# Ten unread products on TensorE between the opening's spectrum and the first steps back

## The chip, the cores and the metric

The kernel runs on one core of a Trainium2 chip. The time is that of one execution on the device, in microseconds (us). Before the change five runs gave a median of 1884.59 us (1883.99 to 1885.54). A profile is one further execution with the hardware profiler on; its own time is given beside it.

## The reference

A spectral filter over a sequence, followed by a feed-forward block with a softmax-like gate:

```python
# x (8, 3136, 256), filt_r and filt_i (1569, 256)
X = np.fft.rfft(x, axis=1)
Y = X * (filt_r + 1j * filt_i)[None, :, :]
x = np.fft.irfft(Y, n=3136, axis=1).reshape(25088, 256)

h = x @ w_in                                    # (25088, 1024)
sm = exp(h - max(h)) / (sum(exp(h - max(h))) + 1e-9)
solu = h * sm
ln = (solu - mean(solu)) / sqrt(var(solu) + 1e-6) * g_ln
out = ln @ w_out                                # (25088, 256)
```

All of it is done in 32-bit floats.

## The kernel before, in words

The transform of length 3136 is split as 49 x 64, and each part is done as matrix products with constant tables. For each of the 8 sequences ("entries") there are four steps:

- **first** (L171, product L177, tile `pa`): a table `wf_t` times rows of `x`. ACT copies the result from PSUM to `t` (L180), and DMAs store it to a DRAM scratch `d1`.
- **forward** (L199, product L203, `pb`): rows fetched back from `d1` are multiplied with the table `de`. DVE and ACT then multiply with the filter in `multiply` (L207), which leaves the product tile `p` in `prods`.
- **inverse** (L227, product L233, `pc`): `de` again, times `p`. ACT copies the result to `g` (L236), and `store` (L238) sends it by a DMA of the POOL queue to a second DRAM scratch `d2`.
- **back** (L253, product L258, `py`): `fetch_back` (L245) brings a chunk of `d2` into a tile `t` by two DMAs of the SP queue (L145, L146: 96 rows and 4 rows). A group of four products of 100 rows and 98 columns with the table `wi_t` fills one PSUM tile, which ACT copies into `y` (L261). A chunk gives two groups, one for each half of the 256 channels.

Then the feed-forward block works on blocks of 128 tokens: `h` (L415) from `y` and `w_in_sb`, maximum, exponential and gate on DVE and ACT, a transposition by DVE and DMA, and `po` (L475) with `w_out_sb`.

The program has two stages. The **opening** (L267 to L369) handles entries 0 and 1 alone: all of their first steps, then a loop over 25 units of the spectrum (L354), in which unit i + 1 is started before unit i is inverted, then the back steps of entry 0 in 8 chunks, 16 groups (L362). On DVE it also converts the weights from 64-bit words (L280). The **main stage** (L549 on) runs over 196 token blocks in an order written out by hand, with the transforms of the other entries spread between the blocks; it keeps TensorE full nearly all of its length. Its first rows of `x`, `x_1` and `x_2` among them, are asked for on the SP queue behind the last chunk of the opening's back steps.

PSUM is divided into pools by tag. `h` (two slots of two banks) holds `pa` and `pb` of the opening and `h` of the main stage. `t` (two slots of one bank) holds `pc`, `py` and the main stage's `pa`. So a `py` group needs one of two slots, and gets it when ACT has copied the group before last. In the opening the framework derives the waits from the tiles; instructions of one engine run in the order in which they are queued there. The SP queue, too, is in order: chunks 0 to 5 of the back steps have buffers at once, chunks 6 and 7 wait until chunks 0 and 1 have been used by `py`, and the main stage's rows are queued behind them.

The last store of `d2` in the opening must land before the first chunk can be read back, since every chunk takes rows from all 25 units.

Of the kernel before, what the change touches and what calls it, by code (L numbers as in the profile page):

```python
# [9 lines left out]
FP32 = mybir.dt.float32  # L10
# [7 lines left out]
P = 128  # L18
# [62 lines left out]
def kernel(  # L81
# [10 lines left out]
    nc = tc.nc  # L92
# [5 lines left out]
    def pool(name, bufs, space=None, stack=ctx):  # L98
        kw = {} if space is None else {"space": space}
        return stack.enter_context(tc.tile_pool(name=name, bufs=bufs, **kw))  # L100
# [3 lines left out]
    ps_h = pool("ps_h", 2, PSUM)  # L104
# [19 lines left out]
    de = consts.tile([P, NS, 2, P], FP32, name="de")  # L124
# [142 lines left out]
    with ExitStack() as st:  # L267
# [61 lines left out]
        sp = Spectrum(0, pools, resident)  # L329
        raws = {}  # L330

        def begin(j):
            raws[j] = load_words(weights[j][1], j)
# [13 lines left out]
        def start(i):  # L347
            sp.fetch(i)
            sp.fetch_filter(i)
            sp.forward(i, ps_h.tile([P, 2, 512], FP32, name=f"pb_0_{i}", tag="h").rearrange(  # L350
                "p a (b c) -> p (a b) c", c=C)[:, 0:2, :])

        start(0)
        for i in range(NS):  # L354
            sp.multiply(i)
            if i + 1 < NS:
                start(i + 1)
            sp.inverse(i, nc.scalar.copy)
            sp.store(i, nc.gpsimd.dma_start)
        for j in (4, 5):  # L360
            begin(j)
        for ch in range(NH // NCH):  # L362
# [140 lines left out]
    for g in range(NS // NG):  # L503
        for k, filt in enumerate((filt_r, filt_i)):
            for half in range(2):
                loads[g].append(lambda filt=filt, half=half, k=k, g=g: nc.gpsimd.dma_start(
                    out=f_dram[NG * g:NG * g + NG, 32 * half:32 * half + 32, k, :].rearrange(
                        "s p c -> p s c"),
# [4 lines left out]
    for n in range(1, len(GROUPS)):  # L513
        entries, first_at, spectrum_at = GROUPS[n]
        sp = Spectrum(n, pools, load_filter)
# [15 lines left out]
    for e in range(1, B):  # L531

        start, end = -(-S * (e - 1) // P) + (3 if e == 3 else 1), S * e // P - 1
# [67 lines left out]
```

## Time and profile before

| | |
|---|---|
| median of 5 runs | 1884.59 us (1883.99 to 1885.54) |
| the profiled execution | 1884.83 us |
| its span, first to last instruction | 1882.9 us |
| mean granted clock of TensorE | 0.974 |
| PE busy | 1806.0 us, 96% of the span |
| DVE, ACT, POOL busy | 1112.0, 817.2, 456.5 us |
| DMA | 300.77 MB, 160 GB/s in the mean |
| all `py` products (L258) | 147.8 us |
| all `pa` products (L177) | 144.5 us |

PE is TensorE's row of products, PEld its row of weight loads, which lies beside the products. A 32-bit product appears as two instructions, so a count of x8 on PE is four products of the program. The page cuts the span into 40 slices and gives a digit for each: for an engine the tenths of the slice in which it was busy, for PEclk the clock that TensorE was granted, in tenths of full speed. At half clock every product takes twice as long, and PE counts as busy all that time: a full PE row doesn't say that PE runs at its best, the clock row must be read with it. The ends of products are modelled, and two that follow each other overlap by some 0.2 us; so the pace is read from start to start.

The waits name, for an engine and a line, what ended its idle time. The chain of waits goes back from the last instruction to whatever released each step. A question for stretches of time gives each engine's busy time between two moments, with the granted clock and the share of time in which the 16 DMA engines were busy.

### The profile page before, as it was taken

How to read it: one execution, taken by the hardware profiler on the slowest of the kernel's cores; microseconds unless marked ns; L12 is line 12 of the kernel's file. 1: busy time of each engine (PE TensorE's matmuls, PEld its weight loads, DVE VectorE, ACT ScalarE, POOL GpSimd, SP SyncE). 2: the span in 40 equal slices, each digit the busy share in tenths (PEclk: the TensorE clock that was granted, in tenths of full speed). 3: DMA queues.
4: the chain of work that ended last, by engine and by line, in shares of the span. 5: the costliest groups of instructions: out<-in, count | busy, mean ns of one | idle time of the engine just before them, and what ended most of it. 6: DMA issues, size and time to landing. Idle time of an engine off the chain costs nothing.

```text
span 1882.9 us, 21235 instructions
## 1 busy us (share of the span) xinstructions
PE 1806.0 (96%) x6500; PEld 1167.5 (62%) x6500; DVE 1112.0 (59%) x1778; ACT 817.2 (43%) x1329; POOL 456.5 (24%) x1306
## 2 busy tenths in 40 slices
PE   6678799999999999999999999999999999999997
PEld 1126456666666666666666666666767666666665
DVE  0792455566665655566676655566665655666663
ACT  2373345545545534354545444444444343333331
POOL 3241243332333221132232121213222011110110
PEclk9795899999999999999999999999999999999999
DMA  9875489877787765666657656466675534434434
GB/s 284 255 232 153 142 225 251 233 195 173 185 210 192 200 151 140 144 149 164 169 148 175 157 121 158 103 158 166 155 179 114 116 89 114 112 83 103 101 90 101
DMA packets 314575, 300.77 MB, mean 160 GB/s; under 512 B 27601, under 2 KB 278994, under 8 KB 314464
## 3 DMA queue, kind: packets, MB, share of 16 engines
q1 hardware_dynamic: 283904, 206.69, 47.2%
q0 software_dynamic: 28768, 86.45, 15.3%
q10 hardware_dynamic: 1792, 6.29, 0.9%
q8 instruction: 53, 0.87, 0.2%
q14 instruction: 58, 0.48, 0.1%
HBM read 118.44 MB, written 81.40 MB: 106 GB/s over the span
## 4 chain that ended last, share of the span: by engine, by line
PE 90%; DMA 3%; issue 2%; POOL 1%; DVE 1%; ACT 1%; SPq 0%; POOLq 0%; DVEq 0%; ACTq 0%
PE po L475 36%; PE h L415 35%; PE py L258 7%; PE pa L177 5%; PE pb L203 4%; PE pc L233 3%; DMA x<-in_x_dram 1%; POOL d L241 1%; DMA d<-t 1%; DMA t<-d 1%; DVE nmax L420 0%; ACT e L423 0%; DVE solu L438 0%; ACT t L180 0%; POOL f L310 0%
## 5 line engine op out<-in xcount | busy, mean ns | idle before, releaser
L475 PE MATMUL po<-w_out_sb,solu_t 128*128 128x256 f32 x3136 | 711.8, 380 | 4.5 <-DVE ot L483 4.5
L415 PE MATMUL h<-w_in_sb,y 128*128 128x512 f32 x1568 | 710.1, 596 | 0.0
L475 PEld LDWEIGHTS po<-w_out_sb,solu_t 128*128 128x128 f32 x3136 | 591.7, 190 | 137.9 <-issue 57.0
L420 DVE TENSOR_REDUCE nmax<-h 128x1 f32<-128x1024 f32 x196 | 239.8, 1223 | 455.2 <-PE h L415 455.2
L415 PEld LDWEIGHTS h<-w_in_sb,y 128*128 128x128 f32 x1568 | 295.1, 191 | 317.0 <-issue 306.4
L423 ACT ACTIVATE e<-h,nmax 128x1024 f32<-128x1024 f32 x196 | 218.6, 1115 | 605.8 <-DVE nmax L420 605.8
L440 ACT ACTIVATE e<-solu,nmu 128x1024 f32<-128x1024 f32 x196 | 225.0, 1148 | 293.2 <-DVE solu L438 287.1
L438 DVE SCALAR_TENSOR_TENSOR solu<-e,rsum,h 128x1024 f32<-128x1024 f32 x196 | 251.0, 1280 | 7.1 <-DVE rsum L435 0.3
L448 DVE STREAM_TRANSPOSE turn<-solu 128x1024 f32<-128x1024 f32 x196 | 242.0, 1235 | 0.0
L241 POOL DMA_DIRECT2D d<-g x101 | 76.0, 753 | 565.9 <-ACT g L236 555.5
L258 PEld LDWEIGHTS py<-wi_t,t 100*128 100x128 f32 x1024 | 148.0, 215 | 59.8 <-issue 41.6
L177 PE MATMUL pa<-x,wf_t 98*100 98x512 f32 x256 | 144.5, 675 | 22.9 <-DMA x<-in_x_dram 17.6
L258 PE MATMUL py<-wi_t,t 100*128 100x98 f32 x1024 | 147.8, 297 | 16.6 <-DMA t<-d 9.3
L467 POOL COPY rs_t<-rs 32x1 f32<-32x1 f32 x784 | 141.7, 181 | 35.7
L483 DVE TENSOR_SCALAR ot<-po,rs_t 128x256 f32<-128x256 f32 x196 | 94.5, 482 | 82.3 <-PE po L475 70.5
L222 DVE TENSOR_TENSOR p<-pb,f 128x512 f32<-128x512 f32 (+1 forms) x101 | 69.2, 685 | 124.2 <-ACT i L215 122.8
L203 PE MATMUL pb<-t,de 128*128 128x512 f32 (+1 forms) x250 | 105.9, 522 | 16.8 <-DMA t<-d 15.8
L261 ACT COPY y<-py 128x392 f32<-128x392 f32 x128 | 106.9, 835 | 32.0 <-PE py L258 31.9
L461 POOL TENSOR_SCALAR rs<-var 128x4 f32<-128x4 f32 x49 | 9.7, 197 | 455.3 <-ACT e L440 453.4
L233 PE MATMUL pc<-p,de 128*128 128x512 f32 (+1 forms) x250 | 103.8, 512 | 10.7 <-DVE p L224 9.2
L177 PEld LDWEIGHTS pa<-x,wf_t 98*100 98x100 f32 x256 | 46.2, 187 | 87.6 <-issue 67.1
L180 ACT COPY t<-pa 100x512 f32<-100x512 f32 (+1 forms) x112 | 71.2, 641 | 63.9 <-PE pa L177 57.1
(51 smaller groups left out, 853.0 us busy)
## 6 DMA issues: line engine op xcount, KB each, us to landing
solu_t<-turn SPq DMA_DIRECT2D x784, 128.0 KB
t<-d SPq DMA_DIRECT2D x99, 256.0 KB
d<-g POOLq DMA_DIRECT2D x99, 256.0 KB, 4.0
out_dram<-ot SPq DMA_DIRECT2D x196, 128.0 KB
x<-in_x_dram SPq DMA_DIRECT2D x64, 384.0 KB
t<-d SPq DMA_DIRECT2D x64, 384.0 KB
d<-t POOLq DMA_DIRECT2D x48, 384.0 KB, 5.0
f<-f_dram POOLq DMA_DIRECT2D x104, 128.0 KB, 4.2
```

What stands on the lines that cost most here:

```text
L177: nc.tensor.matmul(out=ps[0:NK, j], lhsT=wf_t, rhs=self.xs[i][0:NR, 2 * u:2 * u + 2, :], start=True, stop=True)
L203: nc.tensor.matmul(out=ps[:, w * j:w * j + w, :], lhsT=de[:, s + j, 0, :], rhs=t2[:, w * j:w * j + w, :], start=True, stop=True)
L233: nc.tensor.matmul(out=ps[:, w * j:w * j + w, :], lhsT=de[:, s + j, 1, :], rhs=pt[:, w * j:w * j + w, :], start=True, stop=True)
L258: nc.tensor.matmul(out=psv[:, i, :], lhsT=t4s[e, ch][:, i, cb * P:cb * P + P], rhs=wi_t, start=True, stop=True)
L415: nc.tensor.matmul(out=h[:, half, :], lhsT=y[:, c, P * t:P * t + P], rhs=w_in_sb[:, c, 512 * half:512 * half + 512], start=(c == 0), stop= ...
L420: nc.vector.tensor_reduce(out=nmax, in_=h, axis=AX.X, op=ALU.max, negate=True)
L423: nc.scalar.activation(out=e, in_=h, func=AFT.Exp, bias=nmax, accum_out=esum)
L438: nc.vector.scalar_tensor_tensor(out=solu, in0=e, scalar=rsum, in1=hs.pop(k), op0=ALU.mult, op1=ALU.mult, accum_out=nmu)
L440: nc.scalar.activation(out=e, in_=solu, func=AFT.Square, bias=nmu, scale=-float(DFF), accum_out=variances[g][:, i:i + 1])
L448: nc.vector.transpose(out=turns[g][:, :, i, :], in_=solus.pop(k).rearrange("p (f j) -> p f j", j=32))
L467: nc.gpsimd.tensor_copy(out=rss[g][32 * i:32 * i + 32, c:c + 1], in_=rs[32 * c:32 * c + 32, i:i + 1])
L475: nc.tensor.matmul(out=ps, lhsT=solu_t[:, f, :], rhs=w_out_sb[:, f, :], start=(f == 0), stop=(f == KF - 1))
```

## The change

It keeps a handle on the last product tile of the spectrum loop and, after the loop and before the back steps, issues ten products of the table `de` with that tile, each of 512 columns, each to a tile of the PSUM pool `h`. Nothing reads their results. `sp.prods[i]` is the tile `p` of unit i, which `inverse` removes from the list and multiplies with the other half of `de`.

```diff
@@ -355,8 +355,14 @@
             sp.multiply(i)
             if i + 1 < NS:
                 start(i + 1)
+            last = sp.prods[i]
             sp.inverse(i, nc.scalar.copy)
             sp.store(i, nc.gpsimd.dma_start)
+
+        for j in range(10):
+            idle = ps_h.tile([P, 2, 512], FP32, name=f"idle_{j}", tag="h")
+            nc.tensor.matmul(out=idle[:, 0, :], lhsT=de[:, 0, 0, :],
+                             rhs=last.rearrange("p b c -> p (b c)"), start=True, stop=True)
         for j in (4, 5):
             begin(j)
```

In the changed kernel the ten products are on line 364, and every line behind them has a number six higher (L258 and above keep theirs; L415 becomes L421).

## The prediction

> **What bounds the kernel now.** I read the page first, its slices above all, then the waits of TensorE, the chain of waits, and last the opening in short stretches.
>
> ```profile
> PE   6678799999999999999999999999999999999997
> PEclk9795899999999999999999999999999999999999
> ...
> PE py L258 <- DMA t<-d: 9.3, 1, 9.3
> ...
> 139.38 4.40 DMA d<-g
> 144.73 5.05 DMA t<-d
> 149.92 27.60 PE py L258 x128
> 177.51 6.54 PE pa L177 x8
> ```
>
> The first two lines are slices of 47 us: from the sixth on TensorE is full and its clock is up; in the fourth (141 to 188 us) the clock is half gone. The third line is the wait at issue (us in total, times, longest). The rest is the chain: the last spectrum store lands, the first rows come back, TensorE starts `py` at 149.92 and sets the end from there. From 254.0 on PE is busy 1618 of 1629 us, at clock 1.00. So what `py` starts or ends earlier should reach the end of the kernel undiminished, if the stretch from 184 to 254 us doesn't swallow it.
>
> Now the same place in stretches. Columns: busy us (and count) of PE, PEld, DVE, ACT, POOL, then granted clock, DMA share, GB/s.
>
> ```profile
> 77.83:81.25 3.42, 3.13 (x5) 0.70 (x3) 0.77 (x2) 1.46 (x3) 0.00 (x0) 0.50 0.29 83
> ...
> 139.27:142.68 3.41, 1.10 (x2) 0.30 (x2) 3.41 (x9) 0.59 (x1) 1.60 (x3) 1.00 0.83 256
> 142.68:146.09 3.41, 0.00 (x0) 0.00 (x0) 3.20 (x7) 0.00 (x0) 0.54 (x1) 0.50 0.74 269
> ...
> 26.64:30.05 3.41, 1.93 (x4) 0.58 (x4) 0.00 (x0) 1.60 (x2) 1.34 (x3) 1.00 1.03 381
> 30.05:33.46 3.41, 2.49 (x6) 0.92 (x7) 0.00 (x0) 1.44 (x2) 0.57 (x2) 1.00 1.00 320
> 40.29:43.70 3.41, 1.72 (x4) 0.33 (x2) 0.00 (x0) 1.94 (x2) 0.87 (x2) 1.00 1.05 290
> 43.70:47.12 3.42, 0.00 (x0) 0.00 (x0) 0.26 (x1) 0.00 (x0) 0.69 (x2) 0.50 1.00 302
> ...
> 149.92:177.31 27.39, 27.39 (x129) 27.39 (x129) 3.58 (x6) 12.40 (x15) 0.00 (x0) 0.50 0.51 124
> 177.31:183.90 6.59, 6.59 (x10) 2.26 (x10) 0.00 (x0) 2.57 (x4) 1.08 (x2) 0.52 0.27 72
> ```
>
> Cut at 142.68 plus or minus multiples of 3.413 us, nearly the whole opening falls into stretches with one clock each, 1.00 or 0.50. What a stretch did decides the clock of the next: after 1.10 or 1.72 us busy it fell, after 1.93 us or more it stayed. The pause (140.64 to 149.92) drops it at 142.68. The reader is to see the last two lines: all 16 `py` groups, and the four `pa` products behind them, run at half clock, with PE never idle. Those 34 us are the target, not the 9.3 us of waiting.
>
> **Part 1: the ten products.** In the order on TensorE they stand between `pc_24` and the first `py`, and no other engine's order changes. They need `p_24` (ready, since `pc_24` used it) and the PSUM pair `h`, which the last multiply has left. One product of 128x512 advances PE by 0.86 us: four of L415 take 3.44 us from start to start of what follows (207.60 to 211.04). `pc_24` starts at 139.54, so they start at 140.40 and end at 140.40 + 10 x 0.86 = 149.0, 0.9 us before the rows land. Eight of them wait for a PE semaphore of their own, which no row of before shows: at best nothing (the product between covers it), at worst each runs as a lone one, 1.10 us (the row of `pc`), so 11.0 us and an end at 151.4, 1.5 us late. I take 0.86, since `h` pairs streamed like this in L415. Queued behind them is only `py`, which waits for DMA anyway; no DMA, ACT or DVE instruction waits for them, and what later uses `h` (L415) comes 20 us after. Cost 0, with 1.5 us as the far end.
>
> **Part 2: the clock over the pause.** Each stretch now holds at least 2.5 us of products, above the 1.93 us that kept the clock. It is 1.00 at 149.92.
>
> **Part 3: the back steps at full clock.** A group is four products. Later in the trace, alone at clock 1.00:
>
> ```profile
> 256.26 1.11 PE L258 MATMUL py<-wi_t,t 100*128 100x98 f32 x8
> ...
> 257.41 0.84 ACT L261 COPY y<-py 128x392 f32<-128x392 f32 x1 [0.36 <-PE py L258]
> ```
>
> PE moves on after 0.95 us (at 257.21), the copy starts 1.15 us after the group's start and takes 0.83. A PSUM slot freed by ACT starts PE 0.05 us later (256.19 to 256.24). With two slots, a slot's round is 1.15 + 0.83 + 0.05 = 2.03 us for two groups, against 2 x 0.86 = 1.72 for PE alone and 1.66 for ACT: the PSUM round is the new bound. Eight rounds take 16.2 us, so `pa` starts at 166.2 instead of 177.3: 11.1 us. Were PE the bound, 13.8 us: 2.5 more.
>
> Do rows arrive in time? A chunk of 0.40 MB at the 253 GB/s of the full stretches takes 1.6 us, below 2.03. SP issues chunks 6 and 7 when chunks 0 and 1 are used up (153.65 and 157.07 before, about 152.0 and 154.0 now); needed at 162.1 and 164.1, and the landings here took 3.2 to 5.1 us. Behind them on SP are `x_1`, `x_2` and the next `t`, three more times 1.6 us, there by about 163. Nothing is late.
>
> **Part 4: the four `pa`.** At half clock they take 6.59 us until L415 starts. At full clock 4 x 0.86 plus a little PSUM waiting (round 1.15 + 0.59 + 0.05 = 1.79 for two): 3.6 us. That is 3.0 us.
>
> **Sum.** 11.1 + 3.0 = 14.1 us. What is late next is the chain from L415 over `nmax`, `e`, `solu` to ACT's copy of `t`, which makes the pauses at 189 and 213 us (4.6 and 4.4 us); it moves along and stays. The profiled execution took 1884.83 us (span 1882.9, 1.9 around it): 1870.7. The median is 0.24 lower: **1870.5 us**.
>
> [...] The rows kept 1.00 at 1.93 and 2.49 us, so I take the row. It has a weak side: they are of other shapes, and `py` streams only 4 x 98 = 392 columns in a group, where a product of 512 takes the same 0.86 us. If columns count, a group is worth 0.86 x 392 / 512 = 0.66 us in 1.015, 65%, still above the 1.93 / 3.41 = 57% that was kept.
>
> **Rivals.**
> - *The clock falls again inside `py`* (slots, as above). For: `py` alone never lifts it. Against: the 57%. Gain 1.5 us, two windows 3.2: 1881.6 to 1883.3. Chance 0.07.
> - *The later pauses take some back.* From 184 to 254 the mean clock is 0.85, since each of three pauses ends in a cold restart, and a shift by 14.1 us moves them against the 3.41 us grid (4.13 steps). For: the restart at 193.8 was cold for 6.9 us, the one at 217.3 for 10.7. Against: a shift can as well shorten them. One window more in each costs 3 x 1.7 = 5.1: 1875.6. One window less in two: 1867.1. Chance that most is lost: 0.06.
> - *Slower: the products themselves run cold.* If a thin stretch before them falls under about 1.8 us (139.27 less 3.41 had 2.17), the clock drops at 139.3, and if they don't lift it, as `py` doesn't, ten products take 10 x 1.72 = 17.2 us, end at 157.6 and start a cold `py` 7.7 us late: 1892.5. It decides where busy time before the pause drops below 1.8 us. Against: `pb`, of the same shape, lifted the clock at 81.25 after one stretch of 3.13 us. Chance 0.03.
> - *They don't fill the pause*, because they are unread or put elsewhere: excluded by the order on PE.
>
> **How the numbers follow.** The forecast has 0.84, its rivals 0.07, 0.06 and 0.03. The range: down by PE as the bound (2.5) and a shorter restart (1.7) to 1866.3; up by late products (1.5) and two longer restarts (3.4) to 1875.4, which takes in most of the second rival: **1866.3 to 1875.5**. About 0.2% (3.8 us) is what a measurement can tell from no change; the re-fall lies within it. Faster 0.90, same 0.07, slower 0.03.
>
> **What would show it.** Ten L364 rows, 0.86 us apart, from 140.4 to 149.0; clock 1.00 from 140 to 189 less shift; `py` at 1.0 us a group with ACT named before it; `pa` from about 166 us, first L415 near 169.8; from 254 less 14 on the same work in the same time. The forecast is wrong if the clock is 0.50 anywhere in `py`, if `py` waits for DMA again, or if L415 starts 14 us earlier and the stretch to 254 grows.

## The result and the profile after

| | before | after |
|---|---|---|
| median | 1884.54 us (46 runs) | 1874.71 us (26 runs) |
| range | 1879.32 to 1889.66 us | 1869.98 to 1890.6 us |
| profiled execution | 1884.83 us | 1884.31 us |
| its span | 1882.9 us | 1882.4 us |

The ratio is 0.996, with a 95% interval of 0.995 to 0.9971: faster, by 0.4%. The medians lie 9.8 us apart where 14.1 were forecast; the ratio, which compares the runs as a whole, gives 7.5 us. More telling than either is that the times of the changed kernel fall into two clusters. Sixteen of the 26 lie between 1869.98 and 1876.84 us, ten between 1880.41 and 1890.6. With twelve more executions of the same kernel (below) it is 24 with a median of 1873.3 us and 14 with a median of 1882.6. The mean granted clock tells these 38 apart: 0.981 to 0.986 in the lower, 0.974 to 0.980 in the upper.

The profiled execution is of the upper cluster. First its slices, from the page:

```profile
PE   5579899999999999999999999999999999999997
PEclk9797899999999999999999999999999999999999
```

The fourth slice has a full PE, so the pause is filled, but its clock is only 0.7. The timeline of TensorE shows why (start, length, instruction, count, and in brackets the idle time before it and what ended it):

```profile
139.76 1.10 PE L233 MATMUL pc<-p,de 128*128 128x512 f32 x2 [1.09 <-DVE p L224]
140.70 8.75 PE L364 MATMUL idle<-p,de 128*128 128x512 f32 x20
150.70 26.05 PE L258 MATMUL py<-wi_t,t 100*128 100x98 f32 x128 [1.26 <-DMA t<-d]
176.55 5.47 PE L177 MATMUL pa<-x,wf_t 98*100 98x512 f32 x8
181.85 3.60 PE L421 MATMUL h<-w_in_sb,y 128*128 128x512 f32 x8
```

The ten products run as forecast. A pause of 1.26 us is left, and then the back steps take 26.05 us instead of 27.60, most of them at half clock. The same place in stretches of 3.41 us (busy us of PE, PEld, DVE, ACT, POOL, then clock, DMA share, GB/s):

```profile
146.17:149.58 3.41, 3.27 (x8) 1.14 (x6) 2.69 (x6) 0.00 (x0) 0.00 (x0) 1.00 1.06 267
149.58:152.99 3.41, 2.25 (x18) 2.11 (x19) 3.20 (x7) 1.10 (x2) 0.00 (x0) 1.00 1.00 217
152.99:156.41 3.42, 3.42 (x18) 3.42 (x18) 1.04 (x2) 1.54 (x3) 0.00 (x0) 0.50 1.04 279
```

The pause and the first groups of `py` share the second stretch. TensorE was busy for 2.25 us of it, more than the 1.93 us that had kept the clock in the opening, and still the clock fell at its end.

### The profile page after: what moved, and what is told of

Same layout as the page of the kernel before. It is cut to its first block, busy times and chain, and to the rows that moved or that the text cites. A ratio compares the mean times of both kernels' runs of the same rounds, so it can differ in the third digit from the quotient of the medians.

```text
span 1882.4 us, 21275 instructions
## 1 busy us (share of the span) xinstructions
PE 1810.0 (96%) x6520; PEld 1169.1 (62%) x6520; DVE 1112.2 (59%) x1778; ACT 817.0 (43%) x1329; POOL 456.0 (24%) x1306
## 4 chain that ended last, share of the span: by engine, by line
PE 89%; DMA 4%; issue 3%; POOL 1%; DVE 1%; ACT 1%; SPq 0%; POOLq 0%; DVEq 0%; ACTq 0%
PE po L481 36%; PE h L421 35%; PE py L258 7%; PE pa L177 5%; PE pb L203 3%; PE pc L233 3%; DMA x<-in_x_dram 2%; DMA d<-t 1%; POOL d L241 1%; DMA t<-d 1%; ACT t L180 0%; ACT e L429 0%; DVE nmax L426 0%; DVE solu L444 0%; POOL f L310 0%
## 5 line engine op out<-in xcount | busy, mean ns | idle before, releaser
L421 PE MATMUL h<-w_in_sb,y 128*128 128x512 f32 x1568 | 708.9, 595 | 0.0
L421 PEld LDWEIGHTS h<-w_in_sb,y 128*128 128x128 f32 x1568 | 294.7, 191 | 315.7 <-issue 305.2
L258 PEld LDWEIGHTS py<-wi_t,t 100*128 100x128 f32 x1024 | 146.4, 212 | 51.9 <-issue 33.5
L258 PE MATMUL py<-wi_t,t 100*128 100x98 f32 x1024 | 146.3, 294 | 8.6 <-ACT t L180 7.3
```

The lines of the kernel that those rows point to most:

```text
L258: nc.tensor.matmul(out=psv[:, i, :], lhsT=t4s[e, ch][:, i, cb * P:cb * P + P], rhs=wi_t, start=True, stop=True)
L421: nc.tensor.matmul(out=h[:, half, :], lhsT=y[:, c, P * t:P * t + P], rhs=w_in_sb[:, c, 512 * half:512 * half + 512], start=(c == 0), stop= ...
```

## Experiments

Theory A, the thin entry: the clock falls where the rest of the pause and the thin first groups come together in one stretch, so it depends on where the stretches happen to lie. Theory B, thin steps: back steps that wait for PSUM slots are themselves too thin. Theory C: the gain is taken back later.

**The changed kernel again.**

> The changed kernel once more, for a second profile of it. Theory A (thin entry): the clock falls inside the back steps only in executions where the rest of the pause, about 1 us, and the first groups share one 3.41 us stretch; so times come in two clusters, near 1873 us (clock kept) and near 1882 us (clock lost), about 6 in 10 in the lower. Theory B (thin steps): every slot-bound stretch of the back steps is near the limit; then the fall comes at varying places of the back steps and times spread evenly between 1871 and 1884 us. If the profile is of a kept clock, both give back steps of 16 to 17 us; theory C (taken back later) gives that too, but an end less than 11 us earlier.

Twelve executions: eight from 1868.63 to 1874.74 us, four from 1879.8 to 1883.17; ratio 0.9948 (0.9931 to 0.9966). This time the profiled one (1873.73 us) kept its clock. Its timeline of TensorE:

```profile
139.34 1.10 PE L233 MATMUL pc<-p,de 128*128 128x512 f32 x2 [1.09 <-DVE p L224]
140.28 8.75 PE L364 MATMUL idle<-p,de 128*128 128x512 f32 x20
150.25 16.47 PE L258 MATMUL py<-wi_t,t 100*128 100x98 f32 x128 [1.23 <-DMA t<-d]
166.71 3.80 PE L177 MATMUL pa<-x,wf_t 98*100 98x512 f32 x8
170.35 3.60 PE L421 MATMUL h<-w_in_sb,y 128*128 128x512 f32 x8
...
235.59 2.03 PE L258 MATMUL py<-wi_t,t 100*128 100x98 f32 x8 [2.22 <-ACT t L180]
237.41 6.13 PE L481 MATMUL po<-w_out_sb,solu_t 128*128 128x256 f32 x16
```

Here is the forecast's picture: the same pause, 1.23 us, but 16.5 us of back steps (16.2 forecast), 3.6 us of `pa` (3.6 forecast), first L421 13.6 us earlier than before. Its stretches differ in one thing, where the pause lies:

```profile
146.91:150.32 3.41, 2.18 (x6) 0.67 (x4) 3.10 (x7) 0.00 (x0) 0.00 (x0) 1.00 1.05 243
150.32:153.74 3.42, 3.37 (x29) 3.21 (x29) 3.25 (x6) 2.00 (x3) 0.00 (x0) 1.00 1.03 260
153.74:157.15 3.41, 3.36 (x28) 3.03 (x27) 0.10 (x1) 2.96 (x4) 0.00 (x0) 1.00 1.02 267
```

The pause shares its stretch with products of 512 columns. Only 2.18 us were busy there, less than the 2.25 us at which the other execution lost its clock, and the clock stayed. Busy time therefore doesn't tell these two apart; what is streamed may. A group of `py` streams 392 columns where a product of 512 takes the same 0.86 us, so the 2.25 us, 18 instructions of 98 columns each, have by estimate the columns of about 1.5 us of such products. The two stretches of slot-bound `py` behind it keep the clock, which speaks against theory B. That they are slot-bound shows in the row of weight loads, which wait for ACT's copy every second group:

```profile
152.29 1.88 PEld L258 LDWEIGHTS py<-wi_t,t 100*128 100x128 f32 x16 [0.21 <-ACT y L261]
```

For theory C there is something too. L421 starts 13.6 us earlier, the end of the span only 11.1. The last two lines of the timeline show the place: after the third of the later pauses `po` takes 6.13 us, where it took 4.48 before, since the shift put that cold restart differently against the stretches; the other two restarts cost 0.35 us each.

**Seven, nine, thirteen and eighteen products.** Only the number changes:

```diff
-        for j in range(10):
+        for j in range(7):      # 9, 13, 18
```

> Seven products: they end at about 146.7, a pause of 3.5 to 4 us is left. Both theories: the clock falls in almost every execution, 1882 to 1886 us, no cluster near 1873. If the clusters were made by something other than the pause (for example by the opening's row loads), they would stay as with ten.

> Nine products: about 2.1 us of the pause are left, against 1.2 us with ten, 3.6 us with seven and none with thirteen. Theory A, in numbers: a full-clock stretch of 3.41 us must hold columns worth about 1.7 us of products (it was kept at 1.7 and lost at 1.5), and back steps that wait for PSUM slots stream 65% of the time. A stretch of nothing but back steps then holds 2.2 us' worth and can lose 0.8 us to the pause. If the stretches lie anywhere, the share of executions with a lost clock is about the pause over 3.41 us: 35% with ten (measured: 14 of 38), 60% with nine, all with seven, none with thirteen. So with nine: two clusters again, some 6 in 10 near 1882 us, the rest near 1873 us. If the share is as with ten, the length of the pause isn't what decides.

> Thirteen products in place of ten: they end at about 152, after the first rows land, so no pause is left. Theory A: no thin stretch at the entry, the upper cluster goes, nearly all executions near 1874 us (1873 + 1.0 us of overrun). Theory B: the upper cluster stays with the same share, and the median rises by about 1 us.

> Thirteen products once more, since six executions are few: theory A wants none in the upper cluster, all between 1869 and 1878 us, median 1873 to 1874 us. With the share of ten products, two of six would be above 1879 us.

> Eighteen products: they end at about 155.9, some 5.5 us after the first rows have landed. Theory A: no upper cluster, and each product past the end of the pause costs its 0.86 us, so 4.3 us over thirteen, about 1877.5 us. Rival (rows and PSUM copies, once ahead, let the back steps catch up): since chunks are there but a slot's round sets the pace at 2.03 us, nothing can be caught up; if it can, the time stays near 1873 us.

| products | pause left in a profile | below 1878 us | above | ratio |
|---|---|---|---|---|
| 7 | 3.55 us | 0 | 12 | 0.9993 (0.998 to 1.0006) |
| 9 | 1.60 us | 6 | 6 | 0.9968 (0.9945 to 0.9991) |
| 10 | 1.26 and 1.23 us | 24 | 14 | 0.996 and 0.9948 |
| 13 | none | 12 | 0 | 0.9938 (0.9922 to 0.9955) and 0.9943 (0.9929 to 0.9958) |
| 18 | none | 4 | 1 | 0.9961 (0.9947 to 0.9974) |

The share of executions in the upper cluster rises with the pause that is left: none, 14 of 38, 6 of 12, all. (The step from ten to nine alone is within chance.) For nine the expectation was 60%, and the pause in its profile was shorter than supposed. This is theory A's picture; theory B wanted the upper cluster to stay with thirteen products, some 4 of 12 executions, and there are none. The opening's loads and spectrum steps are the same in all of these. With eighteen the fifth execution took 1881.6 us, but its mean clock, 0.982, is more like that of a kept one; what lengthened it is open. With thirteen all twelve are fast, median 1873.0 us, although three more products than ten run; with seven nothing is gained that is clear of noise (the medians lie 2.4 us apart, the ratio's interval includes 1), in spite of 6 us of added activity. With eighteen the median is 1876.8 us, 3.8 above thirteen where 4.3 were expected: the five products past the end of the pause cost nearly their time, some 0.8 us each, and nothing behind them catches up. Its timeline:

```profile
140.89 15.61 PE L364 MATMUL idle<-p,de 128*128 128x512 f32 x36
156.34 16.39 PE L258 MATMUL py<-wi_t,t 100*128 100x98 f32 x128
172.70 3.83 PE L177 MATMUL pa<-x,wf_t 98*100 98x512 f32 x8
```

No wait for rows is left, and the back steps still take 16.4 us: slot rounds set their pace, not data.

**Four PSUM slots for the opening's back steps.**

```diff
-        ps = ps_t.tile([P, 512], FP32, name=f"py_{e}_{ch}_{cb}", tag="t")
+        ps = {"b": ps_b, "t": ps_t, "o": ps_o}[kind].tile(
+            [P, 512], FP32, name=f"py_{e}_{ch}_{cb}", tag=kind)
...
-                back(0, ch, cb, nc.scalar.copy)
+                back(0, ch, cb, nc.scalar.copy, ("t", "tbto"[2 * (ch % 2) + 1])[cb])
```

> Ten products, and the back steps of the opening take four PSUM slots in turn instead of two, so TensorE doesn't wait for ACT's copies there. Theory B: no thin steps, the upper cluster goes; median near 1871 us. Theory A: the entry is as thin as before for its first group, denser after it, so the upper cluster shrinks only in part; where the clock is kept the back steps take 13.8 to 14.2 us instead of 16.2, so the lower cluster moves from 1873 to about 1871 us.

```profile
143.52 8.75 PE L365 MATMUL idle<-p,de 128*128 128x512 f32 x20
153.71 14.50 PE L259 MATMUL py<-wi_t,t 100*128 100x98 f32 x128 [1.44 <-DMA t<-d]
168.05 3.66 PE L177 MATMUL pa<-x,wf_t 98*100 98x512 f32 x8
```

From start to start the back steps take 14.3 us, 2.1 less than with two slots: the slot round was the bound, as the forecast had it. Five of six executions lie between 1869.19 and 1871.71 us, the sixth at 1884.97 with a clock of 0.975. By its clock the sixth lost it, so four slots with ten products don't remove the fall. Six executions are too few to say whether they make it rarer.

**Products in the midst of cold back steps**, to see whether it is their shape that leaves the clock down. The kernel before, with five added products:

```diff
                 back(0, ch, cb, nc.scalar.copy)
+            if ch == 1:
+                t4 = t4s[0, 1]
+                for j in range(5):
+                    idle = ps_h.tile([P, 2, 512], FP32, name=f"idle_{j}", tag="h")
+                    nc.tensor.matmul(out=idle[:, 0, :], lhsT=t4[:, 0, 0:P],
+                                     rhs=t4[:, 0:2, :].rearrange("p n c -> p (n c)"),
+                                     start=True, stop=True)
```

> The kernel before, without the ten products, and with five unread products of 512 columns between the fourth and the fifth group of the back steps, where the clock is at half. Theory A (what counts is how densely columns stream in a stretch; 98 columns in a product are too thin to lift the clock, though not to keep it): the five lift the clock after one or two stretches, the other 12 groups run at 1.0 us each, and L415 starts 3 to 6 us earlier in spite of 6 to 8 us of added products: about 1880 us. Rival (back steps can't hold a full clock, or it is the time since the pause that counts): the clock stays at 0.50 or falls at once, and the time is 1884.5 + 7 to 8.6 = 1892 us.

Nine executions, median 1881.28 us; ratio 0.9981 (0.9971 to 0.999). The timeline, and then two stretches, during the five products and after them:

```profile
147.29 7.12 PE L258 MATMUL py<-wi_t,t 100*128 100x98 f32 x32 [9.13 <-DMA t<-d]
154.20 6.50 PE L370 MATMUL idle<-t 100*128 100x512 f32 x10
160.54 12.25 PE L258 MATMUL py<-wi_t,t 100*128 100x98 f32 x96
...
176.43 3.60 PE L422 MATMUL h<-w_in_sb,y 128*128 128x512 f32 x8
```

```profile
154.85:158.26 3.41, 3.41 (x5) 1.35 (x4) 0.00 (x0) 0.41 (x1) 0.00 (x0) 0.50 0.03 11
158.26:161.68 3.42, 3.42 (x17) 2.08 (x16) 0.00 (x0) 0.07 (x1) 0.00 (x0) 1.00 0.00 0
```

Four groups run cold, 1.73 us each. The stretch that five products of 512 columns fill lifts the clock (0.50 in it, 1.00 behind it), and the twelve groups behind them keep it, at 1.02 us each. From the first group to L422 it is 29.1 us instead of 34.0, although 6.3 us of idle products were added. The rows of these products have 100 partitions like those of `py`; what differs is 512 columns to 98. So back steps can hold a full clock, and it is not the time since the pause that counts.

**Products in the three later pauses alone**, in the kernel before:

```diff
+    def fill(count):
+        idle = psum("b", "fill")
+        for _ in range(count):
+            nc.tensor.matmul(out=idle.rearrange("p a c -> p (a c)"), lhsT=de[:, 0, 0, :],
+                             rhs=w_in_sb[:, 0, 0:512], start=True, stop=True)
+
+    first_of[1].insert(2, lambda: fill(5))
+    first_of[3].insert(2, lambda: fill(5))
+    early[6].insert(2, lambda: fill(3))
```

> The kernel before with unread products of 512 columns in the three later pauses only: five before the first back step of entry 1, five before the third pair of first steps that waits for ACT, three before the next back steps. It tells how much the cold restarts there are worth, which the forecast left as they were. If each of the three restarts loses half of its cold time (3.4, 5.3 and 1.7 us before) and the products fit into the pauses (4.6, 4.4, 2.2 us): about 8 to 10 us, less 0.4 for the third one's overrun, 1875 to 1877 us. If ACT's chain is delayed by them or the clock falls all the same: 1884 us or more.

Median 1874.08 us, ratio 0.9948 (0.9935 to 0.9961). The timeline around the first of the three:

```profile
186.43 1.88 PE L177 MATMUL pa<-x,wf_t 98*100 98x512 f32 x4
188.15 4.46 PE L552 MATMUL fill<-w_in_sb,de 128*128 128x512 f32 x10
192.88 2.03 PE L258 MATMUL py<-wi_t,t 100*128 100x98 f32 x16 [0.27 <-ACT t L180]
194.74 3.62 PE L415 MATMUL h<-w_in_sb,y 128*128 128x512 f32 x8
```

A wait of 0.27 us is left, and `py` with L415 takes 5.3 us to the next step instead of 8.6 (193.78 to 202.43 before). The back steps of the opening stay cold in this kernel (27.60 us), so these 10.8 us are a gain of their own.

**All together**: thirteen products, four slots, and the three fills.

> Thirteen products in the first pause, four PSUM slots for the opening's back steps, and the products in the three later pauses. If the parts add up: 1873 less 2.0 for the slots less 6 to 8 for the restarts, 1863 to 1866 us, in one cluster.

Four executions from 1857.64 to 1861.7 us, median 1859.14; ratio 0.9865 (0.985 to 0.988), so 1.35% faster than the kernel before and clearly below the changed one. The parts add up: thirteen products gave 12.0 and 11.0 us, 11.5 in the mean, the fills 10.8, the slots about 2 (the 2.1 above), together 24.3, where 25.7 were measured. (The 1863 to 1866 us expected had counted only 6 to 8 us for the fills.) In its profile the clock is 1.00 from 130 us to the end:

```profile
130.00:1858.00 1728.00, 1713.23 (x6402) 1128.61 (x6401) 1039.83 (x1658) 761.90 (x1249) 410.49 (x1233) 1.00 0.63 154
```

## Why the prediction was right or wrong

- **The bound** was read rightly: half a clock over `py` and the four `pa`, not the pause. Seven products, which fill two thirds of the pause and leave the clock to fall, gain nothing clear of noise.
- **Part 1** held. The ten products take 0.86 us each, the waits for their own semaphore cost nothing. The pause behind them was put too small: 0.9 us from the pace of the products, against 1.4 in both profiles of the changed kernel. The first rows had come 10.4 us after the last `pc` started in the one trace that was read; in those two it was 10.9, and in the other profiles in which `py` waited for rows 10.2 to 11.5.
- **Part 2 is the step that failed.** It checked the stretches filled with products against 1.93 us busy and took the clock at 149.92 as settled. The stretch that counted is the next one, with the rest of the pause and the first thin groups in it. There only 2.25 us were busy, not at least 2.5, and lost the clock, where 2.18 us of products kept it. The forecast had another measure in hand, columns (65% against 57%), but applied it to steady back steps and not to a stretch with a pause in it. (Its 57% was busy time still: the four instructions in that stretch stream for 4 x 0.43 = 1.72 us, 50%.)
- **Parts 3 and 4** held where the clock was kept: 16.5 us for 16.2, 3.6 for 3.6, with the PSUM round as the bound, as the copies named before the weight loads and the test with four slots show. The rows were in time.
- **The first rival**, the clock falling again, had 0.07. It came in 14 of 38 executions, not by short waits for slots alone as the rival had it, but by what is left of the pause; thirteen products remove it with the slots as they are. No run shows its terms, gains of 1.5 and 3.2 us; what the runs showed is the upper cluster, 2.0 us below the kernel before by the medians.
- **The second rival**, later pauses taking some back, is small and real: 2.4 us in the profile with a kept clock (L421 13.6 us earlier, the end 11.1). Most of it is the third restart, 1.65 us, close to the 1.7 us that the forecast took for half a stretch. With rows that came 0.5 us later than supposed that is the way from 1870.5 to the lower cluster's 1873.3.
- **The median** of 1874.71 lies in the range, but that is in part luck: it is a median over two outcomes, of which the lower was the more frequent, and the forecast had nearly all its chance on that one. By the ratio, 0.996 x 1884.5 = 1877.0 us, the runs as a whole lie above the range. (The terms of the range add up to 1875.4 at its upper end, not 1875.5.)
- **The clock within the back steps** was read rightly: before the change 27.4 us of them, with PE never idle, stayed at 0.50. Slot rounds alone kept 1.00 (150.32 to 157.15 in the second profile), and the fall took a pause of 1.3 us in the same stretch.

## What to carry to other kernels

Filling a pause pays by what runs behind it at half clock, so look for long thin work after the pause, and don't go by its busy time alone: here 2.25 us of 98-column products lost the clock, and 2.18 us, nearly all of 512-column products, kept it. Fill the pause wholly, over its spread from one execution to the next: one product too many costs some 0.8 us here, 1.2 us of pause left open cost some 9 us in over a third of the executions. When one profile decides, look at the cluster that it came from before reading it; and before settling for one pause, ask what every pause in the trace costs in clock.

## What the runs showed of the hardware that was not expected

The 3.41 us stretches don't lie at the same place of the kernel in every execution: in one profile of the changed kernel a stretch ended 2.29 us after the first back step's start (152.99 against 150.70), in the other 0.07 us after it (150.32 against 150.25). So the same instructions with nearly the same pause (1.23 and 1.26 us) kept the clock or lost it by where the stretches happened to lie.

Products of 98 columns kept a full clock here, at 1.0 us a group, but never raised it by themselves: 27.4 us of them, PE never idle, stayed at 0.50 (149.92 to 177.31 before), while one stretch of five 512-column products raised it. Nor was 512 columns enough by itself. These are two stretches of `pa` products, which have 98 rows, in the opening of the kernel before:

```profile
50.53:53.94 3.41, 3.41 (x5) 0.99 (x4) 2.80 (x7) 1.01 (x1) 0.56 (x1) 0.50 0.96 234
53.94:57.36 3.42, 3.42 (x5) 1.11 (x4) 3.32 (x8) 1.01 (x1) 0.95 (x2) 0.50 0.77 272
```

PE is full in both, with the same count of the same instruction, yet the clock is still 0.50 behind the first and 1.00 only behind the second. What tells the two apart is not shown: no run here changed rows alone.

Cut on the same grid, the profile of the kernel before has 18 stretches at half clock in which PE was busy all the time. Behind six of them the clock was 1.00, behind twelve still 0.50. Eleven of these twelve held `py` products of 98 columns, for 0.70 us at least; the twelfth is the first of the two above. Of the six, two held `py` products, for 0.16 and 1.95 us, and the other four had only products of 512 columns. So busy time doesn't sort the stretches at half clock, and 98 columns against 512 sorts most of them. At full clock busy time sorts those of that profile from 23.2 us on (up to 1.73 us were followed by 0.50, 1.93 us and more by 1.00), but the 2.25 us that lost the clock in the first profile of the changed kernel don't fit that.
